# Decode attention with a parallel Mish block: the loads of wo, placed between other keys and values

## The chip, the cores and the metric

The kernel runs on one core of a Trainium2 chip. The time is that of the whole execution on the device, in microseconds (us), the median of several runs. The profile is of one execution, with the times of every instruction and of every packet of the transfers.

## What is computed

One decode step for 8 sequences: grouped-query attention over a cache of 8192 keys and values and a dense Mish block, both fed from the same normalised input, are added to the input.

```
xn = layernorm(x)                                   # x: 8 x 512
q  = xn @ wq                                        # 32 heads of 128, 4 heads share a key head
p  = softmax(q . k_cache * 128**-0.5)               # k_cache, v_cache: 8 x 8 x 8192 x 128, float32
A  = (p . v_cache).reshape(8, 4096) @ wo            # wo: 4096 x 512
h  = xn @ w1 + b1                                   # w1: 512 x 1792
Bm = (h * tanh(softplus(h))) @ w2                   # w2: 1792 x 512
out = x + A + Bm
```

All numbers are float32. The keys and the values are 268 MB each, so nearly all that the kernel moves is read once and used once.

## The kernel before

The work is a list of items, each with a load of at most 4 MB and the work on what it loaded. An item is the keys of one sequence and one key head (`load_k`, `k_work`), the values of such a pair (`load_batch`, `v_work`), a quarter of wq, a quarter of wo, w1, or a part of w2. Four sequences of one key head make a pack (there are 16 packs p, with b from 0 to 3 inside a pack). Keys of pack p alternate with values of pack p - 1, since the values need the softmax of the whole pack.

Every load goes to one of four buffers of 4 MB that are used in turn (`BUFS`, lines 67 and 94), also a load that is smaller. So each load waits until the work on the load four places before it is over. All loads of weights, keys and values are issued from the queue of SyncE (SP), in the order of the items, three items ahead of the work (line 711). A load that has to wait holds up all loads behind it in that queue. ScalarE's queue carries only x and b1, at the start; GpSimd issues no transfers.

The order of the instructions on TensorE and VectorE is the order in which the program writes them; lines 723 to 736 chain them. Work that is to come later is put into a list with a count (`after`, line 601), and each `yield` of an item's work calls `step`, which runs what has become due. The work on keys has four such steps (each a quarter of the products, line 353), the work on values two (lines 444 and after it). For a pack the late work is: the largest score (`maximum`), the exponents and their transposition (`weights`), the sums of the exponents (`sums`, line 428), the merging of the values' parts (`merge`, line 471), and, when a key head is complete, `turn` (line 493), which brings the heads' outputs into the layout `oW` for the product with wo.

`outputs` (line 505) multiplies a quarter of wo, 2 MB for two key heads, by `oW`: 64 matrix instructions at line 523 (each product of the program is two instructions in the profile). For the first quarter it also adds x. The first three quarters are accumulated in PSUM and added to `acc` by VectorE. They stand in the list after the values of b = 3 and ahead of the first keys of the next pack, and their work is put off by three steps:

```
            if i > PB and (i - PB + 1) % (2 * NP * PB) == 0 and p < PACKS:
                items.append(wo_item((p - 1) // NP - 1))
```

The last quarter of wo belongs to the end. There, after the last values, w2 is loaded in three parts (2, 1 and 0.5 MB) into one buffer, and the last quarter of wo comes after the first part. Its products and those of w2 (`down`, line 590) go into the same place in PSUM, and the last instruction of VectorE adds `acc` to it.

Of the kernel before, what the change touches and what calls it, by code (L numbers as in the profile page):

```python
# [16 lines left out]
HKV = 8  # L17
# [10 lines left out]
BW = 1024  # L28
# [8 lines left out]
PB = 4  # L37
NP = B // PB
PACKS = HKV * NP
# [22 lines left out]
OR = 4  # L62
# [9 lines left out]
def kernel(  # L72
# [12 lines left out]
    nc = tc.nc  # L85
# [8 lines left out]
    def buffer():  # L94
        return kv.tile([P, NB * BW], F32, name="kv")

    def rows_of(blocks):

        return blocks.rearrange("j p f -> (j p f)").rearrange("(p f) -> p f", p=P)

    def load_rows(blocks):
        src = rows_of(blocks)
        t = buffer()[:, : src.shape[1]]
        nc.sync.dma_start(t, src)
        return t

    def batch_blocks(src, p, b):
        n, hb = divmod(p, NP)
        lo = ((hb * PB + b) * HKV + n) * NB
        return src[lo : lo + NB]  # L110

    def load_batch(src, p, b):
        return load_rows(batch_blocks(src, p, b))

    def load_k(p, b):
        if p > 0:
            return load_batch(kT, p, b)
        t = buffer().rearrange("p (t f) -> p t f", t=NH)
        nc.sync.dma_start(
            t,  # L120
            batch_blocks(kT, p, b)
            .rearrange("(t a) p f -> t (a p f)", t=NH)
            .rearrange("t (p f) -> p t f", p=P),
        )
        return t

    W2_PARTS = ((0, 4), (4, 6), (6, 7))
# [17 lines left out]
    items = []  # L145
# [26 lines left out]
    half = const.tile([P, 2], F32, name="half")  # L172
# [128 lines left out]
    def expand(p):  # L301


        n, hb = divmod(p, NP)
        t = qT[p % QBUFS]
        if p > 0:
            t = t.rearrange("p (b c) -> p b c", b=PB)[:, :, :QB]
            t = t.rearrange("p b (r q) -> p b r q", r=KR)
            q = qc[:, n % 4, :, :, hb * PB : (hb + 1) * PB].rearrange("p r h b -> p b r h")
            for j in range(NB):  # L310
                g, s = divmod(j, NH)
                lo = g * R + s * PB
                nc.vector.tensor_scalar(  # L313
                    t[:, :, :, lo : lo + R - U + 1 : U], q, bsel[:, j : j + 1], None, op0=ALU.mult
                )
            return
        t = t[:, : PB * (QA + 1)].rearrange("p (b c) -> p b c", b=PB)[:, :, :QA]
        t = t.rearrange("p b (r q) -> p b r q", r=KA)
        for a in range(KA):
            rows = slice(P // KA * a, P // KA * (a + 1))  # L320
            g, s = divmod(a, NH)
            lo = g * R + s * PB
            nc.vector.tensor_copy(
                t[rows, :, :, lo : lo + R - U + 1 : U],
                qc0[rows, :, :, :PB].rearrange("p r h b -> p b r h"),
            )
# [3 lines left out]
    def scores(p, b, k):  # L330

        t, sp = qT[p % QBUFS], S[p % 2]
        for c in range(GK // 512):
            cols = slice(c * 512, (c + 1) * 512)
            if p == 0:
                for i in range(KA):
                    w = QA * b + WK * i
                    at = i * BW + c * 512
                    for z in range(NH):
                        nc.tensor.matmul(  # L340
                            sp[WK * z : WK * (z + 1), cols],
                            t[:, w : w + WK],
                            k[:, z, at : at + 512],
                            start=(b == 0 and i == 0),
                            stop=(b == PB - 1 and i == KA - 1),
                        )
                if c == 0:
                    yield
            else:
                for r in range(KR):  # L350
                    w = QB * b + P * r
                    at = r * BW + c * 512
                    nc.tensor.matmul(  # L353
                        sp[:, cols],
                        t[:, w : w + P],
                        k[:, at : at + 512],
                        start=(b == 0 and r == 0),
                        stop=(b == PB - 1 and r == KR - 1),
                    )
                    if r % 4 == 3 and (c, r) != (GK // 512 - 1, KR - 1):  # L360
                        yield
        if b == PB - 1:
            NM[p] = work.tile([P, 1], F32, name="nm")
            nc.vector.tensor_reduce(NM[p], sp, axis=AX.X, op=ALU.max, negate=True)  # L364
            if p == 0:

                nc.gpsimd.memset(t[:, : PB * (QA + 1)], 0.0)
# [58 lines left out]
    def sums(p, lsel):  # L426
        n = REP * PB
        nc.tensor.matmul(  # L428
            M[:, 136 : 136 + n], ones, lsel.rearrange("p h b -> p (h b)"), start=True, stop=True
        )  # L430
        RT[p] = work.tile([P, REP, PB], F32, name="r")
        nc.vector.reciprocal(RT[p].rearrange("p h b -> p (h b)"), M[:, 136 : 136 + n])  # L432
# [69 lines left out]
            to[rows].rearrange("p r h b -> p (r h b)"), M[rows, 384 : 384 + OR * 2 * B]  # L502
        )

    def outputs(n, w):

        last = n == HKV - 2
        to = H[:, :P] if last else M[:, 256:384]
        if n == 0:

            for g in range(G):
                nc.tensor.matmul(
                    to[Q * g : Q * g + B, :],
                    ident[:B, :B],
                    x_sb[:, g * P : (g + 1) * P],
                    start=True,
                    stop=False,
                )
        for r in range(OR):
            for h in range(2):  # L520
                for g in range(G):
                    at = r * BW + h * D + g * P
                    nc.tensor.matmul(  # L523
                        to[Q * g : Q * g + B, :],
                        oW[n][:, r, h, :],
                        w[:, at : at + P],
                        start=(r == 0 and h == 0 and 0 < n and not last),
                        stop=(r == OR - 1 and h == 1 and not last),
                    )
        if n == 0:  # L530
            nc.vector.tensor_copy(acc, to)
        elif not last:
            nc.vector.tensor_add(acc, to, acc)
# [67 lines left out]
    def after(k, f):  # L601
        late.append([k, f])
# [36 lines left out]
    def k_work(p, b):  # L639
        def work_on(t):  # L640
            if (p, b) == (0, 0):
                expand(0)
            yield from scores(p, b, t)
            if b == 0 and p + 1 < PACKS:
                expand(p + 1)
            if b == PB - 1:

                def largest():
                    maximum(p)
                    after(1, exponents)  # L650

                def exponents():
                    lsel = weights(p)
                    after(3 if p < PACKS - 1 else 2, lambda: sums(p, lsel))

                after(3 if 0 < p < PACKS - 1 else 2, largest)
            yield

        return work_on
# [8 lines left out]

    def wo_work(n):
        def work_on(t):  # L670
            if n == HKV - 2:
                after(1, lambda: outputs(n, t))
                yield
            else:
                after(3, lambda: outputs(n, t))

        return work_on

    def w2_work(parts):
        def work_on(t):  # L680
            for lo, hi in parts:
                down(lo, hi, t)
                yield

        return work_on

    def wo_item(n):
        return lambda: load_rows(wo[n * 2 : n * 2 + 4]), wo_work(n)
# [3 lines left out]
    for i in range(PB * PACKS + PB):  # L692
        p, b = divmod(i, PB)
        if p < PACKS:

            if b == 2 and p % (2 * NP) == 2 and p < PACKS - NP:
                items.append(wq_item(p // (2 * NP) + 1))
            if i == 2:
                items.append((lambda: load_rows(w1), w1_work))
            items.append((lambda p=p, b=b: load_k(p, b), k_work(p, b)))  # L700
        if p > 0:
            items.append((lambda p=p, b=b: load_batch(v, p - 1, b), v_work(p - 1, b)))
            if i > PB and (i - PB + 1) % (2 * NP * PB) == 0 and p < PACKS:
                items.append(wo_item((p - 1) // NP - 1))
    for part in W2_PARTS:
        items.append((lambda part=part: load_w2([part]), w2_work([part])))
        if part is W2_PARTS[0]:
            items.append(wo_item(HKV - 2))

    tiles = {}  # L710
    for i in range(-AHEAD, len(items)):
# [63 lines left out]
```

## Time and profile before

| | |
|---|---|
| median of 3 runs | 1320.9 us (1320.76 to 1320.94) |
| the profiled execution | 1320.14 us, its span 1318.4 us |
| granted TensorE clock, mean | 0.973 of full speed |
| bytes read from memory | 561.01 MB, 426 GB/s over the span |
| loads of keys, of values | 64 and 64, 4096 KB each |
| loads of wq, of wo | 4 and 4, 2048 KB each |
| one matrix instruction on keys (line 353) | 607 ns long, 1920 of them busy for 872.2 us |
| one matrix instruction on values (line 444) | 607 ns long, 2048 of them busy for 241.5 us |

The span is the time from the first to the last instruction. Instructions of TensorE overlap, so the busy time of a group is less than their number times the mean. In the lines of the profile, PE is TensorE, DVE is VectorE, ACT is ScalarE and SP is SyncE, whose queue issues the loads; `kv` is any of the four buffers, and what stands behind the arrow is read: `kv<-in_wo` is a load of a part of wo. A line such as `PE s L353` is the group of instructions of line 353 on TensorE that write `s`. What stands in square brackets at the end of a line of a timeline is the idle time of the engine before it, and what ended it. In a table of stretches, each engine has its busy time and the count of its instructions; the last three columns are the granted clock, the busy share of the 16 transfer engines and the rate in GB/s.

### The profile page before, as it was taken

To read this page: it belongs to the slowest core of one execution; us is meant where nothing else is said; L and a number is where in the kernel's file an instruction comes from. 1 tells how busy PE (TensorE), PEld (TensorE's weight loads), DVE (VectorE), ACT (ScalarE), POOL (GpSimd) and SP (SyncE) were. 2 spreads that over 40 slices of the span, in tenths; PEclk is the share of its full clock that TensorE was granted. 3 is DMA by queue.
4 is the path that set the end of the run, shared out by engine and by line. 5 is a ranking of instruction groups with operands and counts; after the bars stand their busy time and mean duration, and the time that the engine had idled before them with its cause. 6 is when DMAs were issued, how large, how long until landed. Compare 5 with 4: busy or idle time off the path is not lost.

```text
span 1318.4 us, 11659 instructions
## 1 busy us (share of the span) xinstructions
PE 1202.5 (91%) x5268; PEld 519.8 (39%) x5268; DVE 271.6 (21%) x679; ACT 42.1 (3%) x71; POOL 8.7 (1%) x10
## 2 busy tenths in 40 slices
PE   4999989999979998999988999899999799999886
PEld 3344344433334434443333434444343343334323
DVE  4240301303012031120302212131120211203021
ACT  1000000000000000000000000000000000000000
POOL 2000000000000000000000000000000000000000
PEclk8999989999989999999998999999999899999988
DMA  9999999999999999999999999999999999999998
GB/s 402 424 431 429 435 429 433 432 428 429 430 430 417 430 430 430 428 432 433 430 433 431 409 426 429 430 430 431 430 430 427 421 421 431 434 431 431 431 430 346
DMA packets 20889, 561.82 MB, mean 426 GB/s; under 512 B 2268, under 2 KB 2400, under 8 KB 2536
## 3 DMA queue, kind: packets, MB, share of 16 engines
q1 hardware_dynamic: 20816, 561.06, 99.3%
q8 instruction: 41, 0.67, 0.2%
q14 instruction: 8, 0.07, 0.0%
q10 hardware_dynamic: 24, 0.02, 0.0%
HBM read 561.01 MB, written 0.07 MB: 426 GB/s over the span
## 4 chain that ended last, share of the span: by engine, by line
PE 57%; DMA 40%; DVE 1%; issue 0%; ACT 0%; ACTq 0%
PE s L353 43%; DMA kv<-in_kT 39%; PE o L444 7%; PE s L340 2%; DMA kv<-in_wo 2%; PE h L288 1%; PE h L546 0%; PE m L493 0%; PE m L523 0%; PE m L471 0%; DVE e L197 0%; PE h L265 0%; PE h L523 0%; PE m L397 0%; DVE qs L278 0%
## 5 line engine op out<-in xcount | busy, mean ns | idle before, releaser
L353 PE MATMUL s<-kv,qT 128*128 128x512 f32 x1920 | 872.2, 607 | 75.0 <-DMA kv<-in_kT 74.9
L353 PEld LDWEIGHTS s<-kv,qT 128*128 128x128 f32 x1920 | 359.7, 193 | 519.7 <-issue 450.1
L444 PE MATMUL o<-kv,pt 128*32 128x512 f32 x2048 | 241.5, 607 | 12.3 <-DVE pt L416 6.3
L454 DVE TENSOR_SCALAR os<-o,isel 128x128 f32<-128x128 f32 x64 | 22.5, 351 | 588.0 <-PE o L444 588.0
L444 PEld LDWEIGHTS o<-kv,pt 128*32 128x32 f32 x2048 | 73.3, 139 | 154.5 <-issue 137.2
L407 ACT ACTIVATE e<-s,nms 128x1024 f32<-128x1024 f32 x32 | 35.3, 1109 | 1179.3 <-DVE nms L401 1179.3
L416 DVE STREAM_TRANSPOSE pt<-e 128x1024 f32<-128x1024 f32 x32 | 63.1, 2010 | 39.5 <-ACT e L407 39.5
L456 DVE SCALAR_TENSOR_TENSOR os<-o,isel,os 128x128 f32<-128x128 f32 x192 | 67.3, 351 | 6.8
L364 DVE TENSOR_REDUCE nm<-s 128x1 f32<-128x1024 f32 x16 | 19.6, 1224 | 209.3 <-PE s L353 208.2
L471 PEld LDWEIGHTS m<-hsel,os 128*128 128x128 f32 x128 | 23.7, 190 | 32.7 <-issue 30.2
L340 PE MATMUL s<-kv,qT 128*64 128x512 f32 x128 | 29.7, 624 | 1.4 <-issue 1.4
L313 DVE TENSOR_SCALAR qT<-qc,bsel 128x128 f32<-128x128 f32 x120 | 30.7, 339 | 0.0
L288 PE MATMUL h<-psel,qs 128*128 128x32 f32 x136 | 19.4, 301 | 4.0 <-DVE qs L278 4.0
L288 PEld LDWEIGHTS h<-psel,qs 128*128 128x128 f32 x136 | 19.5, 223 | 7.6 <-DVE qs L278 4.7
L471 PE MATMUL m<-hsel,os 128*128 128x4 f32 x128 | 18.8, 217 | 0.0
L340 PEld LDWEIGHTS s<-kv,qT 128*64 128x64 f32 x128 | 10.0, 145 | 20.2 <-issue 20.2
L475 DVE TENSOR_TENSOR oT<-m,r 128x16 f32<-128x16 f32 x16 | 2.8, 174 | 60.6 <-PE m L471 60.6
L295 DVE COPY qc<-h 128x256 f32<-128x256 f32 (+1 forms) x9 | 3.7, 409 | 52.2 <-PE h L288 52.2
L211 PE MATMUL m<-ident,e 8*128 8x8 f32 x4 | 0.6, 257 | 12.4 <-DVE e L209 12.4
L278 DVE TENSOR_SCALAR qs<-h 128x1024 f32<-128x1024 f32 (+1 forms) x9 | 10.4, 1159 | 3.8 <-PE h L265 3.8
L432 DVE RECIPROCAL r<-m 128x16 f32<-128x16 f32 x16 | 4.1, 257 | 26.9 <-PE m L428 26.9
L265 PE MATMUL h<-kv,xnT 128*8 128x128 f32 x256 | 9.4, 309 | 0.0
(95 smaller groups left out, 152.9 us busy)
## 6 DMA issues: line engine op xcount, KB each, us to landing
kv<-in_kT SPq DMA_DIRECT2D x64, 4096.0 KB, 24.6
kv<-in_v SPq DMA_DIRECT2D x64, 4096.0 KB, 28.6
kv<-in_wq SPq DMA_DIRECT2D x4, 2048.0 KB, 19.1
kv<-in_wo SPq DMA_DIRECT2D x4, 2048.0 KB, 19.9
kv<-in_w SPq DMA_DIRECT2D x1, 3584.0 KB, 35.4
kv<-in_w SPq DMA_DIRECT2D x1, 2048.0 KB
kv<-in_w SPq DMA_DIRECT2D x1, 1024.0 KB, 22.0
kv<-in_w SPq DMA_DIRECT2D x1, 512.0 KB, 22.8
```

Of the source, the lines that this page charges most:

```text
L278: nc.vector.tensor_scalar_mul(qs, q_at[n % 2] .rearrange("p (i r o) -> p r o i", r=k, o=1) .to_broadcast([P, k, copies, DH // k]), DH**-0.5,)
L288: nc.tensor.matmul(H[:, r * R : (r + 1) * R], qs[:, r].rearrange("p g i -> p (g i)"), psel.rearrange("p h b -> p (h b)"), start=True, stop ...
L313: nc.vector.tensor_scalar(t[:, :, :, lo : lo + R - U + 1 : U], q, bsel[:, j : j + 1], None, op0=ALU.mult)
L340: nc.tensor.matmul(sp[WK * z : WK * (z + 1), cols], t[:, w : w + WK], k[:, z, at : at + 512], start=(b == 0 and i == 0), stop=(b == PB - 1 ...
L353: nc.tensor.matmul(sp[:, cols], t[:, w : w + P], k[:, at : at + 512], start=(b == 0 and r == 0), stop=(b == PB - 1 and r == KR - 1),)
L364: nc.vector.tensor_reduce(NM[p], sp, axis=AX.X, op=ALU.max, negate=True)
L407: nc.scalar.activation(e[:, :, s, :], S[p % 2].rearrange("p (t f) -> p t f", t=TG), AF.Exp, bias=nms[:, s : s + 1], accum_out=l[:, s : s + 1],
L416: nc.vector.transpose(pt.rearrange("p (m t r) -> p t m r", m=TW, t=TG)[:, half * i : half * (i + 1)], e.rearrange("p t s (q m) -> p t m (s ...
L444: nc.tensor.matmul(o[Q * c : Q * (c + 1), :], PT[p][:, W4 * R * j + b : W4 * R * (j + 1) : PB], vt[:, 512 * j : 512 * (j + 1)], start=(k = ...
L454: nc.vector.tensor_scalar(os, o[:, :DH], isel[:, 0:1], None, op0=ALU.mult)
L456: nc.vector.scalar_tensor_tensor(os, o[:, DH * i : DH * (i + 1)], isel[:, i : i + 1], os, op0=ALU.mult, op1=ALU.add,)
L471: nc.tensor.matmul(M[:, at : at + REP], OS.pop((p, b)), hsel, start=True, stop=True)
```

## The change

The three loads of wo in the loop move by one place: they come after the first keys of the next pack and ahead of the values behind these. Their products are no longer put off by three steps, but follow in the item itself, after those keys. The last quarter of wo is loaded in two halves of 1 MB (`wo_part`), into one buffer: the first half after the first part of w2, the second after the second part. `outputs` gets the range of the rows that it multiplies, so the products of a half are done when that half is there. The items at the end are now: w2 (2 MB), wo (1 MB), w2 (1 MB), wo (1 MB), w2 (0.5 MB). Each column's sum is formed in the same order within wo and within w2.

```diff
-    def outputs(n, w):
+    def outputs(n, w, lo=0, hi=OR):
...
-        for r in range(OR):
+        for r in range(lo, hi):
...
     def wo_work(n):
         def work_on(t):
-            if n == HKV - 2:
-                after(1, lambda: outputs(n, t))
-                yield
-            else:
-                after(3, lambda: outputs(n, t))
+            after(1, lambda: outputs(n, t))
+            yield
...
+    wo_sb = []
+
+    def wo_part(k):
+
+        half = slice(k * OR // 2 * BW, (k + 1) * OR // 2 * BW)
+
+        def load():
+            if k == 0:
+                wo_sb.append(buffer()[:, : OR * BW])
+            nc.sync.dma_start(wo_sb[0][:, half], rows_of(wo[HKV * 2 - 4 :])[:, half])
+            return wo_sb[0]
+
+        def work_on(t):
+            after(1, lambda: outputs(HKV - 2, t, k * OR // 2, (k + 1) * OR // 2))
+            yield
+
+        return load, work_on
...
             items.append((lambda p=p, b=b: load_k(p, b), k_work(p, b)))
+            if i > PB and (i - PB) % (2 * NP * PB) == 0:
+
+                items.append(wo_item((p - 1) // NP - 2))
         if p > 0:
             items.append((lambda p=p, b=b: load_batch(v, p - 1, b), v_work(p - 1, b)))
-            if i > PB and (i - PB + 1) % (2 * NP * PB) == 0 and p < PACKS:
-                items.append(wo_item((p - 1) // NP - 1))
+    wo_parts = [wo_part(0), wo_part(1)]
     for part in W2_PARTS:
         items.append((lambda part=part: load_w2([part]), w2_work([part])))
-        if part is W2_PARTS[0]:
-            items.append(wo_item(HKV - 2))
+        if len(wo_parts):
+            items.append(wo_parts.pop(0))
```

## The prediction

> **What bounds the kernel now.** I read the engine rows first, then the transfer rows, the chain of waits, the waits of SP's queue, stretches cut around the slices in which the rate falls, and the timelines of one stretch and of the tail.
>
> ```profile
> PE 1202.5 (91%) x5268; PEld 519.8 (39%) x5268; DVE 271.6 (21%) x679; ACT 42.1 (3%) x71; POOL 8.7 (1%) x10
> ...
> GB/s 402 424 431 429 435 429 433 432 428 429 430 430 417 430 430 430 428 432 433 430 433 431 409 426 429 430 430 431 430 430 427 421 421 431 434 431 431 431 430 346
> ...
> q1 hardware_dynamic: 20816, 561.06, 99.3%
> ...
> PE 57%; DMA 40%; DVE 1%; issue 0%; ACT 0%; ACTq 0%
> ```
>
> TensorE and the transfers are both near full, but the transfers lead: 561 MB pass at about 430 GB/s in every slice, except the first, the last and three places (417; 409 and 426; 421 and 421). Where TensorE waits, it is for keys (74.9 us before the scores, line 353). So a microsecond in which the transfer engines run dry is a microsecond of the end, unless another one was there to lose. The three places are the three loads of wo inside the loop:
>
> ```profile
> SPq L104 <- PE m L523: 65.9, 3, 22.7
> ```
> ```profile
> 404.00:409.00 5.00, 5.00 (x72) 3.11 (x65) 2.26 (x9) 0.00 (x0) 0.00 (x0) 1.00 0.87 338
> ...
> 727.00:733.00 6.00, 6.00 (x79) 3.52 (x81) 2.25 (x9) 0.00 (x0) 0.00 (x0) 1.00 0.84 328
> ...
> 1051.00:1057.00 6.00, 6.00 (x79) 3.49 (x78) 2.25 (x9) 0.00 (x0) 0.00 (x0) 1.00 0.85 328
> ```
>
> The first line: three times SP waits some 22 us for the products with wo (line 523) before it may issue the next load. The stretches (last two columns: share of the transfer engines, GB/s) show what that does. Against 430 GB/s they lose 5 x (1 - 338/430) = 1.07, 6 x (1 - 328/430) = 1.42 and 1.42 us: 3.9 us together. The timelines of the third place, first SP's queue, then TensorE's:
>
> ```profile
> 1007.13 0.33 SPq L104 DMA_DIRECT2D kv<-in_wo  x1
> 1010.76 0.33 SPq L104 DMA_DIRECT2D kv<-in_kT  x1
> 1026.58 0.33 SPq L104 DMA_DIRECT2D kv<-in_v  x1
> 1030.21 0.33 SPq L104 DMA_DIRECT2D kv<-in_kT  x1
> 1053.35 0.33 SPq L104 DMA_DIRECT2D kv<-in_v  x1
> 1056.95 0.33 SPq L104 DMA_DIRECT2D kv<-in_kT  x1
> ```
> ```profile
> 1036.77 5.94 PE L353 MATMUL s<-kv,qT 128*128 128x512 f32 x8 [6.42 <-DMA kv<-in_kT]
> ...
> 1051.36 1.93 PE L523 MATMUL m<-kv,oW 128*8 128x128 f32 x64
> 1053.22 3.70 PE L353 MATMUL s<-kv,qT 128*128 128x512 f32 x8
> ```
>
> wo comes ahead of the next keys, TensorE stands idle 6.42 us for these, and wo lies in one of the four buffers until three quarters of those keys are used. The next values are issued only then, at 1053.35, when the engines have begun to run dry. And the tail:
>
> ```profile
> 1310.62 3.31 PE L523 MATMUL h<-kv,oW 128*8 128x128 f32 x64 [0.84 <-DMA kv<-in_wo]
> 1313.67 1.86 PE L590 MATMUL h<-kv,aT 128*8 128x128 f32 x48
> ```
>
> The last wo lands at 1290.55 + 19.93 = 1310.49 and the two small parts of w2 at 1290.9 + 22.0 = 1312.9 and 1291.4 + 22.8 = 1314.2; 3.31 us of products with wo stand before those with w2, so TensorE ends at 1315.5, 1.3 us after the last byte.
>
> **The change, part by part.** *The three moved loads.* Nothing is added: the same 64 matrix instructions (72 for the first, with x) and the same addition on VectorE, now after the four quarters of the keys. What moves is which buffer each load waits for, the one of four loads earlier:
>
> - The keys (call them K) no longer follow wo. wo took 2.10 MB / 430 = 4.9 us of the transfer engines, so K lands 4.9 us earlier: 1031.8 at the third place. TensorE's idle time before K at the three places is 6.39, 4.72 and 6.42 us, so K's products start 4.9, 4.7 and 4.9 us earlier. On SP, K is issued in wo's old place (1007.13) and wo in K's (1010.76); both lie over 9 us ahead of the bytes, which hides it.
> - K's products took 1036.77 to 1056.98, 20.2 us. They lose wo's 1.9 us, and about 2.2 us more: their first eight rows took 5.94 us after the long idle time, 3.70 without one. K ends at about 1031.9 + 16.1 = 1048.0.
> - The next values now wait for the end of K, not for wo at three quarters. Behind that wait stand in SP's queue the following keys (which wait for wo, 1048.0 + 1.9 = 1049.9 instead of 1056.95) and all later loads. The values are issued at 1048.0 instead of 1053.35, 5 us earlier. The engines begin to run dry at about 1052 (GB/s falls there), and the first bytes follow an issue after about 1 us, so there are some 3 us to spare. The same sum gives about 401 and 724 at the other places, against 405 and 728.
> - VectorE: the copy or addition into acc comes after the reciprocal of the sums instead of before it, 0.3 us on an engine that is 21% busy; nothing waits for it. The values' products begin after wo's 1.9 us; the values land at 1046.4, ahead of that, and the keys after them only near 1056, so TensorE's next idle time covers the 1.9 us.
>
> So the three dips should close. What is that worth? Above: 3.9 us, if all sixteen transfer engines had lost alike. Below: a load has landed when its slowest engine is done, and the engines ahead run dry first. From the values before a dip to the values after it (two loads) the landings lie 399.4 to 419.6, 723.0 to 742.8, 1046.4 to 1066.7 apart, 20.2, 19.8 and 20.3 us, against 19.4 in an undisturbed place (1144.9 to 1164.3): 0.8 + 0.4 + 0.9 = 2.1 us. The landings release TensorE, yet the dips also bring the engines level again, and this is a loss that returns as a later spread. I take the middle, 3.0 us, since neither row is nearer.
>
> *The tail.* The bytes before the second half of wo are the same as before the second small part of w2 until now, so it lands at 1312.9, plus 0.1 for smaller packets (below): 1313.0. The first half and a part of w2 are done by then: TensorE is free of the turn of the heads at 1309.8. Then 32 rows at 3.31 / 64 = 52 ns take 1.65 us, to 1314.7, and the last 16 rows of w2 at 1.86 / 48 = 39 ns take 0.6 us: 1315.3, a gain of 0.2. If the rows go at the 1.93 / 64 = 30 ns that the same 64 rows take inside the loop, they end at 1314.0, the last part of w2 lands at 1314.3 and TensorE ends at 1314.9, a gain of 0.6. After an idle wait the slower row is nearer: 0.3 us. Below: the split could make the transfers longer. The trace holds packets of 16 KB at 614 ns and of 8 KB at 313 ns in this stretch, so 1 MB more in small packets costs each engine 16 x 313 - 8 x 614 = 96 ns; that is the 0.1 used.
>
> The small parts of w2 land 2.4 and 1.3 us after what stands before them, which is their bytes at the full rate; an extra transfer in a full queue so costs nothing more. The Trainium skill, "DMA: Bandwidth & Descriptors", section "Anatomy of one DMA", counts about 2.0 us fixed for each transfer, by which one more would cost 2 us at the end and the gain would shrink to 1.3 us; that figure is for transfers issued from GpSimd, and these rows from SP don't show it.
>
> Sum: -3.0 - 0.3 = -3.3 us. The profiled execution has a span of 1318.4 us and a time of 1320.14, 0.8 below the median of 1320.9. The span becomes 1315.1, its execution 1316.8, the median 1317.6.
>
> **The rivals.**
> - *The slowest transfer engine decides (no change, 0.12).* If the same engine is last at every dip, it never ran dry, and what the others win is only a wider spread. Then the tail's 0.3 us is left and a little more: 1320.4. For it: the share stays at 0.84 to 0.87 in the dips, so some engines work throughout. Against: the landings themselves come 2.1 us late.
> - *All comes back (faster, 0.10).* The whole 3.9 us and a tail without slow rows, 0.6, and a little of the slower refill around the stretches (426 in the slice behind 409): 4.9 us, 1316.0. Nothing shows that the spread of the engines vanishes.
> - *The later wait decides (slower, 0.07).* The values now wait for all of K. If K started no earlier, they would be issued at 1036.77 + 20.2 - 1.9 = 1055.1, 1.75 us later than now; three times that is 5.2 us: 1320.9 + 5.2 - 0.3 = 1325.8. It decides as soon as K starts less than 1.75 us earlier. Against: the idle time before K is 4.72 us at the least, and the transfer that filled it goes behind K.
> - *The split costs a transfer's fixed time (no change, 0.07).* A gap between transfers of the tail as long as a small one's landing distance (1.3 to 2.4 us), say 2.0: 3.3 - 2.0 = 1.3 us gained, 1319.6. Against: the landings in a full queue above.
>
> **How the numbers follow.** A change of 0.2% (2.6 us, about what a measurement of this kernel tells from none) ends at 1318.3. My forecast has 0.64, with its own range from 1316.4 (3.9 + 0.6) to 1318.8 (2.1 + 0.1, less 0.1 for the packets); about 0.52 of it lies beyond 1318.3. Faster: 0.52 + 0.10 = 0.62. Same: 0.12 + 0.12 + 0.07 = 0.31. Slower: 0.07. The range of 1315.7 to 1319.8 leaves out the slowest engine's case and the later wait, 0.19.
>
> **What would show it.** Right: the stretches around the three wo loads keep 425 GB/s or more; SP no longer waits 22 us for wo's products; TensorE's idle time before K falls from 6.4 us to under 2, and K's first eight rows take 3.7 us; the last wo products take under 2 us and the end follows the last landing by about 1 us. Wrong: dips at other places, values issued after the engines have run dry, full rate everywhere and yet the same end (the slowest engine), or a gap between the last small loads.

## The result and the profile after

The changed kernel takes 1318.04 us (median of 17 runs), the kernel before 1320.94 us, so 2.9 us less. The ratio over all these runs is 0.9981, with a 95% interval from 0.9974 to 0.9987, a gain of 1.7 to 3.4 us. The forecast was 1317.6 us. The gain, 0.19% by that ratio and 0.22% by the two medians, lies at the bound of 0.2% that the prediction drew between faster and the same. The profiled execution has a span of 1316.5 us instead of 1318.4. One run of an experiment below (products one step later) took 2506 us, nearly twice the others, and the median given there leaves it out.

The rate of the transfers in 40 slices, the same three stretches as before (last two columns: share of the transfer engines, GB/s) and what is left of SP's waits for products with wo, now line 524:

```profile
GB/s 402 420 431 431 431 431 430 430 430 430 431 431 433 430 429 432 429 430 433 430 431 429 431 433 428 435 429 434 431 430 430 428 431 430 430 430 432 430 432 324
```
```profile
404.00:409.00 5.00, 3.49 (x36) 0.97 (x28) 1.62 (x5) 0.00 (x0) 0.00 (x0) 1.00 1.00 423
727.00:733.00 6.00, 3.42 (x30) 1.11 (x23) 1.40 (x4) 0.00 (x0) 0.00 (x0) 0.97 1.02 434
1051.00:1057.00 6.00, 2.54 (x16) 0.86 (x9) 1.40 (x4) 0.00 (x0) 0.00 (x0) 0.99 1.02 434
```
```profile
SPq L104 <- PE m L524: 6.4, 3, 2.4
```

The three dips are gone. SP still waits three times for wo's products, 2.4 us at the most instead of 22.7, because the wait for the end of the keys now stands in front. The third place, first SP's queue, then TensorE's timeline (in brackets: idle time before, and what ended it):

```profile
1005.68 0.33 SPq L104 DMA_DIRECT2D kv<-in_kT  x1
1009.31 0.33 SPq L104 DMA_DIRECT2D kv<-in_wo  x1
...
1046.27 0.33 SPq L104 DMA_DIRECT2D kv<-in_v  x1
1048.71 0.33 SPq L104 DMA_DIRECT2D kv<-in_kT  x1
```
```profile
1030.41 3.67 PE L353 MATMUL s<-kv,qT 128*128 128x512 f32 x8 [1.51 <-DMA kv<-in_kT]
...
1046.72 1.93 PE L524 MATMUL m<-kv,oW 128*8 128x128 f32 x64 [0.35 <-DVE r L432]
```

The keys' products start after 1.51 us of waiting instead of 6.42, their first eight rows take 3.67 us instead of 5.94, and the next values are issued at 1046.27 instead of 1053.35. A new wait of 0.35 us stands before wo's products, for the reciprocal of the sums on VectorE; the transfers hide it.

Now the end of the kernel. Both kernels in the same three stretches, before and after:

```profile
1290.00:1300.00 10.00, 4.64 (x42) 1.35 (x34) 2.81 (x8) 0.00 (x0) 0.00 (x0) 0.87 0.97 416
1300.00:1305.00 5.00, 4.29 (x22) 1.12 (x26) 0.00 (x0) 0.00 (x0) 0.00 (x0) 0.58 1.00 423
1305.00:1311.00 6.00, 4.89 (x114) 3.59 (x110) 1.80 (x6) 0.00 (x0) 0.00 (x0) 1.00 0.97 408
```
```profile
1290.00:1300.00 10.00, 5.79 (x38) 1.44 (x34) 1.40 (x4) 0.00 (x0) 0.00 (x0) 0.84 0.98 416
1300.00:1305.00 5.00, 5.00 (x42) 1.45 (x37) 0.00 (x0) 0.00 (x0) 0.00 (x0) 0.73 0.95 392
1305.00:1311.00 6.00, 4.98 (x150) 4.29 (x138) 1.81 (x6) 0.00 (x0) 0.00 (x0) 1.00 0.57 236
```

The last 6 us before 1311 run at 236 GB/s and a share of 0.57 in the changed kernel, at 408 GB/s and 0.97 before. Seven of the sixteen transfer engines have finished their part of all loads by 1306 us, the other nine work on, the last of them until 1312.7, and the kernel waits for those. By the packets of the trace, the bytes up to the end of the last values have been started 3.6 us earlier than before (1294.8 against 1298.5), but the last values land only 1.4 us earlier (1299.2 against 1300.7), and the last part of w2 1.1 us (1313.1 against 1314.2).

This can be followed through the run. The trace does not name the transfer engines, but loads of wq and wo have packets of 16 KB and the others of 32 KB, and a packet starts when the one before it on its engine ends; so each engine shows when it comes to a load of 2 MB. Between the first and the last engine there lie, at the six such loads after the first 100 us: before 2.9, 3.5, 2.5, 3.7, 2.1 and 3.5 us, changed 2.2, 3.4, 3.4, 4.8, 5.9 and 6.5 us. The trace also has sixteen landings for each load, by their number one for each engine. Between the first and the last of them the kernel before has 3.6 us ahead of its first dip and 2.1 behind it, 4.0 and 2.0 at the second, 3.4 and 1.7 at the third, and by the packets at least six engines were busy throughout each dip. So each dip stopped the engines that were ahead until the others had caught up. Without dips nothing does: at the last loads of the changed kernel 8.3 us lie between the first landing and the last.

### The profile page after: what moved, and what is told of

Read it like the earlier page. It is cut to its first block, busy times and chain, and to the rows that moved or that the text cites. A ratio compares the mean times of both kernels' runs of the same rounds, so it can differ in the third digit from the quotient of the medians.

```text
span 1316.5 us, 11660 instructions
## 1 busy us (share of the span) xinstructions
PE 1201.3 (91%) x5268; PEld 519.5 (39%) x5268; DVE 272.4 (21%) x679; ACT 42.1 (3%) x71; POOL 8.7 (1%) x10
## 4 chain that ended last, share of the span: by engine, by line
PE 54%; DMA 43%; DVE 2%; issue 0%; ACT 0%; SPq 0%; ACTq 0%
PE s L353 42%; DMA kv<-in_kT 41%; PE o L444 7%; PE s L340 2%; DMA kv<-in_w 2%; PE h L288 1%; PE h L547 0%; DVE e L197 0%; PE m L471 0%; PE m L493 0%; PE h L265 0%; DVE qs L278 0%; PE m L397 0%; ACT e L407 0%; DVE pt L416 0%
```

## The experiments

Two theories. A: the dips cost all engines alike, so what the rate lost there (3.9 us) comes back. B: the engine that is last decides; it hardly ran dry in the dips, which mainly levelled the engines, so less comes back.

**The loop's three loads alone.** The changed kernel with the tail of before:

```diff
-        if len(wo_parts):
-            items.append(wo_parts.pop(0))
+        if part is W2_PARTS[0]:
+            items.append(wo_item(HKV - 2))
```

> The kernel before with the three loads of wo inside the loop moved, and the tail as before. Theory A (the dips cost every transfer engine alike): the 3.9 us that the dips lost come back, 1320.9 - 3.9 = 1317.0 us, and the landings come as much earlier as the mean of the packets does. Theory B (the transfer engine that is last decides; it hardly ran dry in the dips, and the dips only let it catch up): the last values land 1.4 us earlier, as in the profile of the changed kernel (1299.2 against 1300.7), while the engines drift further apart: about 1319.5 us. In both the three dips are gone.

Measured: 1317.76 us against 1320.74 for the kernel before in the same runs, 0.9982 (0.9973 to 0.9991). Within the scatter of the runs this is the whole gain of the change. The last values land at 1298.7, 2.0 us earlier than before, while their bytes have been started 4.1 us earlier (1294.35 against 1298.47): in these two profiles half of what the dips lost comes back at the landings, which lies between the theories. A's 1317.0 lies just outside the interval, B's 1319.5 just inside its other end, so the times alone don't choose. One thing B's figure left out: the last products end 0.7 us after the last landing here and 1.3 us in the profile of before (see the next ones).

**The tail alone.** The kernel before with the last quarter of wo in two halves (`wo_part` and the range of `outputs` as in the change, left out here):

```diff
...
-        if part is W2_PARTS[0]:
-            items.append(wo_item(HKV - 2))
+        if len(wo_parts):
+            items.append(wo_parts.pop(0))
```

> The kernel before with the last part of wo in two halves, and the loop's loads where they were. Both theories: the landings stay, and the end follows the last landing by 0.6 us less, as the two profiles show (1315.57 - 1314.24 = 1.33 against 1313.83 - 1313.11 = 0.72): 1320.3 us. The prediction had 0.3 us. If the split costs a transfer's fixed time, the last landings come 1 to 2 us later and the kernel is slower than before.

Measured: 1320.16 us against 1320.74, 0.9996 (0.9987 to 1.0005). This does not tell the 0.6 us from nothing. For the tail I put the changed kernel and the kernel of the first experiment on one chip:

> The changed kernel itself, beside the next two on one chip. By its earlier runs 1318.0 us. Both theories say the same of it; it is the measure for the two others.

> Once more the kernel with the loop's three loads of wo moved and the last quarter of wo in one load, now on the same chip as the changed kernel. If the halves are worth the 0.3 us of the prediction: 1318.3 us. If they are worth nothing while TensorE is at full clock, as the first profile of this kernel says (the end follows the last landing by 0.71 us in both): 1318.0 us, the same as the changed kernel.

Measured: 1318.27 us (0.9982, 0.9973 to 0.9991) with the halves, 1317.85 us (0.9981, 0.9972 to 0.9990) without. The halves bring nothing that shows. TensorE's tail without the halves, from the second of these:

```profile
1308.60 1.93 PE L524 MATMUL h<-kv,oW 128*8 128x128 f32 x64 [0.91 <-DMA kv<-in_wo]
1311.02 1.06 PE L591 MATMUL h<-kv,aT 128*8 128x128 f32 x32 [0.48 <-DMA kv<-in_w]
1312.28 0.62 PE L591 MATMUL h<-kv,aT 128*8 128x128 f32 x16 [0.20 <-DMA kv<-in_w]
```

and with them, from the changed kernel's profile:

```profile
1308.63 1.06 PE L524 MATMUL h<-kv,oW 128*8 128x128 f32 x32 [0.32 <-DVE oW L501]
1309.51 1.06 PE L591 MATMUL h<-kv,aT 128*8 128x128 f32 x32
1311.89 1.06 PE L524 MATMUL h<-kv,oW 128*8 128x128 f32 x32 [1.33 <-DMA kv<-in_wo]
1313.16 0.62 PE L591 MATMUL h<-kv,aT 128*8 128x128 f32 x16 [0.20 <-DMA kv<-in_w]
```

In both the last part of w2 is waited for and 0.62 us of products follow it. All of wo's products take 1.93 us in one piece and are over before the next part lands. The 3.31 us that the profile of before shows for them stand in a stretch in which TensorE's granted clock was 0.50 (1311 to 1314 us). In the two profiles above it was 1.00 there, and in every other kernel here but one (the one with other rows, below, at 0.50 again) they take 1.93 us too, or 1.06 for a half.

**Products one step earlier, loads where they were.** In the kernel before:

```diff
-                after(3, lambda: outputs(n, t))
+                after(2, lambda: after(0, lambda: outputs(n, t)))
...
         for f in due:
             f()
+        now = [f for k, f in late if k <= 0]
+        late[:] = [e for e in late if e[0] > 0]
+        for f in now:
+            f()
```

> The kernel before with the products of the loop's three loads of wo one step earlier, after half of the keys and just behind the turn of the heads; no load moves. The next values are issued some 3.7 us earlier, about 1049.7 instead of 1053.35 at the third place, so the dips should close although the keys still land behind wo. TensorE waits up to 1 us at each place for the copy of the turned heads; the transfers hide that. Theory A: 1317.0 us. Theory B: 1319.5 us, and the engines drift apart from place to place as in the changed kernel (from 2.2 us between the first and the last engine at the second load of wq to 6.5 us at the third load of wo), where before they stood at 2.1 to 3.7 us.

Measured: 1321.92 us, 1.0009 (1.0000 to 1.0018). The test missed its aim: the dips stayed, 279, 344 and 273 GB/s in the three stretches.

```profile
1048.36 0.93 PE L493 MATMUL m<-oT,ident 128*32 128x16 f32 x16
1052.25 1.93 PE L523 MATMUL m<-kv,oW 128*8 128x128 f32 x64 [2.96 <-DVE oW L501]
```

TensorE waits 2.96 us for VectorE's copy of the turned heads, which stands behind two transpositions of the exponents (3.92 us). The next values are issued at 1054.25, no earlier than before. What follows for this program: wo's buffer can't be freed earlier by moving its products alone; the load has to move, or VectorE's order.

**Products one step later, loads where they were.**

```diff
-                after(3, lambda: outputs(n, t))
+                after(4, lambda: outputs(n, t))
```

> The kernel before with the products of the loop's three loads of wo one step later, after all of the keys; no load moves. The next values are issued about 3.6 us later, at 1057.0 instead of 1053.35 at the third place. Theory A: each of the dips costs 3.6 us more, 10.9 together: 1331.8 us. Theory B: until now the last engine was busy until about 1055.6; it now stands idle until the bytes come, 1 us after the issue, so each dip costs only about 2.4 us more, 7.2 together: 1328.1 us, and all engines start level after each dip.

Measured: 1323.29 us, 1.0020 (1.0011 to 1.0029), 2.6 us more than before: both theories were far off, for a reason that they share. The delay was not 3.6 us. From the start of the keys' products to the next issue it is 1058.28 - 1040.73 = 17.6 us here and 1053.35 - 1036.77 = 16.6 us before: the keys' last quarter (3.6 us) is added, but wo's products (1.9 us) no longer stand before it, and the first rows were less slow (5.37 us against 5.94). The landings of the two values around a dip lie 22.6, 22.3 and 21.4 us apart, 8.0 us more than 3 x 19.44 undisturbed; before, 2.1 us more. Of the 5.9 us between these, 3.9 us reach the end of the same two profiles (spans of 1322.3 and 1318.4 us) and 2.6 us the medians. So even the landings around a dip count too much. That the levelled engines give part of it back is the likely reason, but this run doesn't show it.

**One dip put back.** The changed kernel with the third load of wo in its old place:

```diff
-            after(1, lambda: outputs(n, t))
-            yield
+            if n == HKV - 4:
+                after(3, lambda: outputs(n, t))
+            else:
+                after(1, lambda: outputs(n, t))
+                yield
...
-            if i > PB and (i - PB) % (2 * NP * PB) == 0:
+            if i > PB and (i - PB) % (2 * NP * PB) == 0 and p < 13:
...
+            if (p, b) == (12, 3):
+                items.append(wo_item(HKV - 4))
```

> The changed kernel with the third of the loop's loads of wo back in its old place, ahead of the keys and with its products after three quarters of them. The third dip returns. Theory A: it costs what the rate loses there, 1.4 us: 1319.4 us. Theory B: with the engines 6.5 us apart at that place the last one never runs dry; the dip stops only those ahead, costs nothing at the end and leaves the engines level: 1318.0 us, with about 2 to 3 us between the first and the last engine at the end in place of 8, and the full rate until the last microseconds.

Measured: 1318.33 us, 0.9985 (0.9976 to 0.9993), beside 1318.27 for the changed kernel on the same chip. The times alone don't exclude A's 1.4 us, the two intervals being 1.1 us wide to either side; the profile decides. The stretch of the dip and the end, from this kernel:

```profile
1051.00:1057.00 6.00, 6.00 (x50) 2.75 (x42) 2.52 (x10) 0.00 (x0) 0.00 (x0) 1.00 0.90 367
```
```profile
1300.00:1305.00 5.00, 5.00 (x26) 1.31 (x22) 0.00 (x0) 0.00 (x0) 0.00 (x0) 0.50 0.96 397
1305.00:1311.00 6.00, 5.41 (x138) 4.00 (x134) 1.80 (x6) 0.00 (x0) 0.00 (x0) 1.00 0.92 381
```

and the end of the changed kernel beside it:

```profile
1300.00:1305.00 5.00, 5.00 (x26) 1.36 (x30) 0.00 (x0) 0.00 (x0) 0.00 (x0) 0.50 1.00 414
1305.00:1311.00 6.00, 5.41 (x122) 3.69 (x118) 1.80 (x6) 0.00 (x0) 0.00 (x0) 0.95 0.60 249
```

The dip is back (367 GB/s), and the bytes up to the last values are started 1.7 us later (1296.9 against 1295.1), yet these land 0.3 us earlier (1299.6 against 1299.9), and the rate holds at 381 GB/s until 1311. By the packets at least eight of the sixteen engines were busy throughout the dip. Between the first and the last landing of a load lie 6.9 us ahead of it and 2.0 us behind it, and 3.1 us at the last loads, against 7.9 in the changed kernel. The dip stopped only engines that were ahead, and levelled them. For this place B is shown.

**Less work for the engines behind?** The changed kernel with other numbers of rows in the last load:

```diff
-            nc.sync.dma_start(w2_sb[0][:, cols], rows_of(w2)[:, cols])
+            for rows in (slice(0, 119), slice(119, P)) if (lo, hi) == W2_PARTS[-1] else (slice(0, P),):
+                nc.sync.dma_start(w2_sb[0][rows, cols], rows_of(w2)[rows, cols])
```

> The changed kernel, with the last 0.5 MB of w2 loaded as 119 rows and 9 rows in place of 128. The Trainium skill, 'DMA: Bandwidth & Descriptors', section 'Why a DMA increments its semaphore by 16 and not by 1', says that a transfer issued from SP runs on the largest number of engines up to 16 that divides its rows, and on the lowest-numbered ones; by that the first is spread over seven engines and the second over nine. The profile of the changed kernel shows seven transfer engines that finish at about 1304.6 us and eight or nine that finish at about 1312.3. If the seven are the lowest-numbered, the engines behind have 8 packets of 161 ns less to do at the end, and the end comes about 1.0 us earlier: 1317.0 us. If the seven lowest-numbered are among those behind, they have 9 packets more, 1.45 us: 1319.5 us. If the rows are spread over all sixteen as before, nothing changes: 1318.0 us. Theory A (all engines alike, nothing to win by shifting work): 1.45 us later.

Measured: 1322.41 us, 1.0012 (1.0003 to 1.0021), on another chip; 4.4 us more than the changed kernel. That is the side on which the engines that got more rows are among those behind, but three times the price expected. In the profile 0.9 us lie ahead of the tail (the last values land at 1300.15 against 1299.23). The second half of wo, which stands ahead of the changed rows in the queue, lands 2.7 us later (1314.57 against 1311.85), and TensorE's last products are slow again (1.90 us for 32 rows, at a granted clock of 0.50). So more than the last rows was late, and which engines are behind the trace does not name: the run settles neither.

**More instruction fetches.** Beside the kernel's own transfers the profile has 41 packets of 16 KB on a queue of instructions, and next to such a packet a packet of keys or values took about 0.5 us longer. The changed kernel with instructions that do nothing:

```diff
     setup()
+    idle = const.tile([P, 8], F32, name="idle")
+    for _ in range(5120):
+        nc.gpsimd.memset(idle[:1, :1], 0.0)
```

> The changed kernel, with 5120 one-element memsets added on GpSimd's queue, which nothing waits for. They make that queue fetch about 20 more blocks of 16 KB of instructions; the profile has 41 such packets (q8), each beside a packet of keys or values that took 0.4 to 0.6 us longer. Theory B with the fetches as the cause of the spread: they fall on the same engines, which lose 20 x 1.1 / 9 = 2.4 us, so the spread between the first and the last engine grows by about that, and the end comes 2.4 us later: 1320.4 us. If the fetches fall on all sixteen engines alike, or are not the cause: 20 x 1.1 / 16 = 1.4 us at the most, and no wider spread: 1318.0 to 1319.4 us.

Measured: 1334.46 us, 1.0103 (1.0089 to 1.0116): 16 us more than the changed kernel, seven times what B had for it. The queues of that kernel:

```profile
q1 hardware_dynamic: 20960, 561.06, 98.1%
q8 instruction: 41, 0.67, 0.2%
q14 instruction: 48, 0.39, 0.1%
```

GpSimd's instructions came as 40 more packets of 8 KB on the other queue of instructions (48 instead of 8), 0.33 MB in all. The landings show where they went. From 142 to 695 us fifteen of the sixteen landings of a load lie within 3 us, and the last one falls further and further behind: by 0.6 us (median of 23 steps from one load to the next) where one of the 8 KB packets lies between, by nothing (12 steps) where none does, the places with gaps left out. So these packets fell on one engine and cost it about 0.6 us each. At the second load of wo it is 13.0 us behind. Three times (near 414, 722 and 746 us) the others ran dry, with one or two engines still busy, since their next loads waited for the buffers; that lost 8.5 us. So the part of B that matters is shown: one engine that is late sets the time of all.

Another 6.9 us have another cause, which the expectation overlooked: by the packets they were lost near 117 us, where all sixteen engines stood still.

```profile
100.00:132.00 32.00, 24.27 (x78) 10.45 (x79) 4.83 (x17) 0.00 (x0) 20.24 (x207) 0.82 0.78 331
```
```profile
L313 DVE TENSOR_SCALAR qT<-qc,bsel 128x128 f32<-128x128 f32 x120 | 30.7, 338 | 17.4 <-POOL idle L709 17.3
```

Nothing waits for the added tile, but a memset that the kernel needs (`qT`, line 367) stood behind some 600 of the added ones in GpSimd's queue and ran only at 103.1 us. VectorE waited 17.3 us for it (second line), TensorE 13.2 us for VectorE, and SP issued the next keys at 120.50 us instead of 104.88. This part has nothing to do with the fetches.

Do the 41 fetches of the kernel itself make its spread? The landings of the changed kernel speak for it. How far all its engines together lie behind the first one changes by 0.03 us from one load to the next where no 16 KB packet of instructions lies between (median of 59 steps), and by 1.6 us where one does (38 steps). That is about the packet itself (1.07 us) and the 0.5 us by which the packet next to it is longer, and the 38 steps make 55 of the 65 us that are added from 76 us to the last values. So most of the drift goes with the fetches, though no run took them away.

## Why the prediction was right, step by step

- *The dips close, by the keys' earlier start and the earlier issue:* right. The values were forecast to be issued at about 401, 724 and 1048, and are issued at 401.4, 723.8 and 1046.3.
- *Nothing waits for VectorE's new order:* wrong by 0.35 us at each place, and without effect on the end.
- *The worth of the dips, 3.0 us, as the middle between 3.9 (the rate) and 2.1 (the landings):* met by the medians, which give 2.7 and 3.0 us for the moved loads alone, but not by the landings. In the profiles of the first experiment the last landings come 2.0 us ahead, which is the lower row; in the four profiles of the changed kernel and of that kernel the last values land between 1298.7 and 1299.9, in those of the kernel before and of the tail alone at 1300.7 and 1301.1, so one pair does not fix the size. The prediction's own reason was right, that the dips level the engines, but I put no number on it and took the middle because neither row was nearer. The returned dip of the experiment above shows that a dip can even be free.
- *The tail, 0.3 us for the two halves:* wrong, it is nothing that shows. The step that failed is the choice of the slower row, 52 ns, from a single execution. The reason given for it, the idle wait before the products, does not hold: the kernel without the halves waits 0.91 us there, the kernel before 0.84, and the same 64 take 1.93 us against 3.31. The slower row stood at a granted clock of 0.50. By the faster row the unsplit products end in 1.93 us, ahead of the next part of w2, and the split has nothing to hide. The shorter end of the changed profile (0.7 us after the last landing, 1.3 before) was no part of the change, since the kernel without the halves has it too. (The 96 ns for smaller packets are those of the 2 MB of wo, not of 1 MB.)
- *An extra transfer in a full queue costs nothing:* nothing in the runs speaks against it. The halves change the time by no more than the runs scatter, and 2 us more at the end would have shown. The figure of the Trainium skill that was weighed there ("DMA: Bandwidth & Descriptors", section "Anatomy of one DMA", about 2.0 us for each transfer issued from GpSimd) is not borne out for this queue of SP.
- *The rivals:* the slowest engine was given 0.12 and no change. As a mechanism it is what the landings show, where only half of the bytes' 4 us came back; as an outcome it was too strong, since the last landings do come earlier. "All comes back" (0.10, 1316.0 us) lies below the interval. The later wait (for all of the keys) did not decide: it ends 7 us earlier than the old one.

The forecast gain of 3.3 us is 0.4 us more than the 2.9 us measured. The tail's 0.3 us did not come, and the loop's 3.0 us did by the medians, while the spans of single profiles give it 2.5 to 2.6 us. That a middle without a reason of its own came out so near is partly luck. The 0.3 to 0.5 us between medians and spans are inside the scatter of the runs and stay open, and so does how often the clock of 0.50 falls on the end of the kernel before.

## What to carry to other kernels

When transfers are the bound, what a gap in the rate costs is not the bytes that it lost: a load is there when its last engine is done, and a gap that only stops the engines ahead is nearly free. Read the landings across the gap beside the rate, as two bounds: for the three dips the time lay between them, for the one returned dip it was nothing. Don't build a term on how long a group took in the one profiled tail when the same group stands elsewhere in the trace at another speed; read the granted clock of both first. And before idle work is added to an engine as a test, see what the kernel itself still wants from that engine's queue.

## What the runs showed of the hardware

Without a gap the sixteen transfer engines drift apart, in the changed kernel from 2.2 us at 172 us to 6.5 us at 1023 us, so that at the end the rate falls to 236 GB/s for the last 6 us while seven have finished. Most of the drift goes with the fetches of instructions: where a packet of 16 KB lay between two loads, the engines together were 1.6 us further behind. Instructions that do nothing are not free on a kernel that is bound by transfers: 5120 memsets on an engine that was otherwise nearly idle cost 16 us. 8.5 us were lost because their fetches fell on one transfer engine, 0.6 us for each, and 6.9 us because a memset that the kernel needs stood behind them.
